# Expert 0's second-layer weights of the last MoE sent last, with two early weight pieces and four operations reordered

## The chip, the cores and the metric

The kernel runs on one core of a Trainium2 chip. The metric is the device time of one execution in microseconds (us); lower is better. The time before is the median of three runs. One further execution was profiled; all rows shown here come from it.

## What is computed

Three layers follow one another. An mLSTM attention runs over 4 batches x 8 heads x 768 tokens with head size 40, and its output is seen as x with 3072 rows and 320 columns. A first mixture of experts works on 32 slots, four for each of 8 experts. A second mixture of experts sends all 3072 rows through all 8 experts and adds them with Sinkhorn weights P.

```python
# first MoE (slots)
d = softmax_over_rows(x @ phi);  slot_input = d.T @ x          # 32 x 320
for e in range(E):
    slot_out[e] = np.maximum(slot_input[e] @ w1[e], 0) @ w2[e]  # 320 -> 1024 -> 320
x = softmax_over_cols(x @ phi) @ slot_out
# second MoE (all rows)
for e in range(E):
    out += P[:, e:e+1] * (np.maximum(x @ m2_w1[e], 0) @ m2_w2[e])
```

Each w1 or w2 of one expert is 320 x 1024 floats, 1.31 MB.

## The kernel before

The kernel has four stages. The attention loop `step` works through 24 tiles of 128 tokens, in an order written out by hand (`ORDER0`, `ORDER`); its last tiles follow `END`, and the way from the last tile to `siT`, the input of the first MoE's slots, follows `TAIL`. Then the first MoE's eight experts run one after another (`up`, `up_t`, `down`). What they give, `soT`, is multiplied with the second MoE's first-layer weights of expert 0 (`s1_p`, the product S); S is scaled by a power of two that comes from its largest magnitude (`pow2_s`) and split into two 16-bit halves (`s1_h`, `s1_l`), and from there on the second MoE runs as matmuls in 16 bits: `g1` gives a first-layer block z and its relu as two halves (hh by ScalarE, hl by VectorE), and `g2` multiplies them with the two 16-bit halves `wh` and `wl` of the second layer's weights. VectorE, ScalarE, GpSimd and TensorE keep the program's order wherever a `manual_schedule` is open. Here `man` holds TensorE throughout, and `man4` holds ScalarE, VectorE and GpSimd from expert 3 of the first MoE on.

The weights all come over SyncE's queue, in program order, into a ring of 15 places (`slot`): two buffers `wa`, three in `big`, two `bigx`, four `bigy`, four `wb`. A DMA is issued once its place is free and an earlier one, eight issues back, has landed. The attention loop sends the first pieces one at a time (`load_w(islice(ahead_parts, 1))`, by the list `WN`), `END` sends the rest of the first eleven matrices (entry `sl20`), and `load_n` sends the others in this order: `w20`, which is expert 0's w2 of the second MoE (n = 11), then the first MoE's matrices 11 to 15 with numbers shifted by one, then `m2w[0]`, the second MoE's w1 of expert 0. Behind them stand the second MoE's weights for experts 1 and 2.

`w20` goes through four steps, each in four quarters of 128 x 640: `amax` (VectorE, line 1091) finds the largest magnitude; `pow2_w` takes it over the partitions on GpSimd (line 1116) and makes a scale by four small VectorE operations (`pow2_b`, lines 1124 to 1132); `prep_a` (ScalarE, line 1149) writes the high half `wh`; and `prep_d` (VectorE, line 1153) the low half `wl`. All of that is woven into the first MoE's loop: `amax` beside experts 1 and 2, the scale at expert 3, and the halves beside experts 3 to 6.

In the code's names, `kk` is a quarter of w2, `kc` one of eight blocks of 128 hidden units, and a quarter of w2 serves two kc. S comes in four column blocks j, each of which serves two kc.

Of the kernel before, what the change touches and what calls it, by code (L numbers as in the profile page):

```python
# [20 lines left out]
def mlstm_moe_kernel(  # L21
# [46 lines left out]
    ORDER0 = "O KT KTa QT E0 E0a QTa E0g ST STd PC PK V E1 E1a E1g G0 DK CB DP US S W0 W1 YB"  # L68
    END = (
        "st sl20 s23 d20 w0 w1 x20 a20 lt4 tv4 n21 y21 g21 i22 v22 u22 i23 r22 v23 n22 y22 g22 x21 a21 q4 u23 x22 a22 r23 n23"  # L70
        " y23 e4 g23"
    )
    PB = [1, 2, 3]
    PD = 3
# [83 lines left out]
    def load_o(i0, i1):  # L158
        for i in range(i0, i1):
            b, c = divmod(i, NCH)  # L160
            nc.sync.dma_start(
                out=xs_(i).rearrange("p (h d) -> p h d", h=H),
                in_=o_gate[b, :, c * L:(c + 1) * L, :].rearrange("h p d -> p h d"),
            )
# [171 lines left out]
    def load_R(p):  # L336
        b, c = divmod(p * CPS, NCH)
        r0 = c // CPS * BH + b * H
        nc.sync.dma_start(out=Rt[p % 2][96:99, :, :], in_=gpd[r0:r0 + H, :, :].rearrange("r a s -> a r s"))
# [292 lines left out]
    def lt_a(gq):  # L632
        nc.scalar.activation(out=ct_all[:, gq], in_=ct_all[:, gq], func=AF.Exp)

    def lt_f(gq):
        ct = ct_all[:, gq]
        sm = late.tile([P, 4, 1], F32, tag="sm", name="sm")
        nc.vector.reduce_sum(out=sm, in_=ct, axis=AX.X)
        nc.vector.tensor_scalar_add(sm, sm, 1e-9)
        nc.vector.reciprocal(sm, sm)  # L640
        nc.vector.tensor_tensor(out=ct, in0=ct, in1=sm.to_broadcast([P, 4, NS]), op=ALU.mult)
# [33 lines left out]
    def load_w(parts):  # L675
        for d, s_ in parts:
            nc.sync.dma_start(out=d, in_=s_)
# [92 lines left out]
    k_a(1, 0, nc.vector)  # L770
    k_a(1, 1, nc.vector)
    load_o(0, 1)
    load_R(1)
    load_v(2)
    load_o(1, 2)
    load_w(islice(ahead_parts, 1))
    load_csa()
    e_g(0, 0)
    pr_k(0)
# [27 lines left out]
    SIG = {s: (s + 2, s + 3) for s in range(4, 22)} | {1: (1, 2), 2: (2, 4), 3: (4, 6)}  # L807
    OL = [4, 5, 6, 7] + list(range(8, NT)) + [NT] * NT
    LO = {i: (OL[i], OL[i + 1]) for i in range(NT + 1)}
    WN = [0, 1] * 8 + [1, 1, 1, 1, 0, 0]  # L810
    for i in range(NT - 2):
        step(i)
    def end():
# [45 lines left out]

    def load_n(n):  # L860

        if n < NRA:
            load_w(m1_parts(n))
        elif n == NRA:
            w20[0] = slot(n)
            load_w(w2_parts(w20[0], m2_w2, 0))
        elif n < 2 * E + 1:
            load_w(m1_parts(n - 1, n))
        elif n == 2 * E + 1:
            m2w[0] = slot(n)  # L870
            load_w(w1_parts(m2w[0], m2_w1, 0))

    for n in range(NRA, NR):
        load_n(n)
# [104 lines left out]
    def wk():  # L979
# [2 lines left out]
            nc.tensor.matmul(wm, ident16, ident16.unsqueeze(1).to_broadcast([P, 4, L]), start=True, stop=True)  # L982

    TAIL = (
        "x23p 0p x23a 0a lp 0d wk ld la mxp ls tp mxd wk tv mbp 1p mbd mba sp lc fwd sd 1a ftp tq ftd 1d te 2p 2a 2d 3p 3a 3d"
        " ltd4 ltf4 ltd lta ltf"
    )
    ops = dict(
        wk=wk, ltd4=lambda: (lt_d(gl - 1), lt_a(gl - 1)), ltf4=lambda: lt_f(gl - 1),
        x23p=lambda: x_p(NT - 1), x23a=lambda: x_a(NT - 1), lp=lambda: lg_p(gl), ld=lambda: lg_d(gl),  # L990
        la=lambda: lg_a(gl, 1), lc=lambda: lg_a(gl, 0), ls=lambda: lg_s(gl),
        tp=lambda: lt_p(gl, (1,)), tq=lambda: lt_p(gl, (0,)), tv=lambda: lt_v(gl, 1), te=lambda: lt_v(gl, 0), mxp=mx_p, mxd=mx_d,
        mbp=mb_p, mbd=mb_d, mba=mb_a, fwd=fw_d, sp=lambda: sl_p(gl), sd=lambda: sl_d(gl), ftp=ft_p, ftd=ft_d,
        ltd=lambda: lt_d(gl), lta=lambda: lt_a(gl), ltf=lambda: lt_f(gl),
    )
    for gq in range(len(cbk)):
        ops[f"{gq}p"] = lambda gq=gq: c_p(gq, *cbk[gq])
# [95 lines left out]
            axis=AX.X, op=ALU.max, apply_absolute_value=True,  # L1093
        )

    SPLIT = ((1, 0), (1, 1), (2, 1))

    def pow2(e, a, mx, later=None):

# [70 lines left out]
    mxg = sm_p.tile([P, 1], F32, name="mxg")  # L1170
    nc.vector.memset(mxg, 0.0)
    sg = sgs[:, 3 * NS:3 * NS + E]
    src2[0] = w20[0].rearrange("p (k d) -> p k d", d=DM)
    up(0)
    for e in range(E - 1):
        if e == 3:

            man4 = tc.manual_schedule(engines={mybir.EngineType.Activation, mybir.EngineType.DVE, mybir.EngineType.Pool})
            man4.__enter__()
        up_t(e)  # L1180
        up(e + 1)
        down(e)
        load_n(NR + 2 * e)
        load_n(NR + 2 * e + 1)
        if e < 3:
            if e < 2:
                c_p(4 + e, psp, "p")
                c_a(4 + e)
                c_d(4 + e)
            if e:  # L1190
                for kk in range(2 * e - 2, 2 * e):
                    amax(0, kk)
        else:
            if e == 3:
                pow2_w(0)
                c_m()
            prep_a(0, e - 3)
            prep_d(0, e - 3)

    def warm2(n):  # L1200
        pw2 = psz.tile([P, TB], F32, tag="z", name="pw2").rearrange("p (a l) -> p a l", a=4)
# [12 lines left out]
        nc.vector.tensor_copy(o, pt[64 * a:64 * a + 64, 2 * NS:3 * NS])  # L1214
    warm2(2)

    Sst = {}

    def s1_p(e):
# [19 lines left out]
    def s1_c(e, j):  # L1239
        s1_h(e, j)  # L1240
        s1_l(e, j)
# [10 lines left out]
    for kt, (o, n) in enumerate(KS):  # L1252
# [2 lines left out]
            start=(kt == 0), stop=(kt == 2), tile_position=(0, 0),  # L1255
        )
    warm2(10)
    pow2_s(0)

    def sg_s():  # L1260
        nc.vector.tensor_reduce(
# [144 lines left out]
    G1K = 3  # L1406

    s1_c(0, 0)
    g1(0, 0)
    s1_h(0, 1)  # L1410
    g1(0, 1)
    s1_l(0, 1)
    warm2(2)
    for kc in range(KF):
        for tt in range(TPB - 1):
            g2(0, tt, kc, kc + 1)
            if tt == 0 and 0 < kc < KF - 2:
                g1(0, kc + 2)
        if kc == 0:
            s1_h(0, 2)  # L1420
            g1(0, 2)
            s1_l(0, 2)
        elif kc == 1:
            s1_c(0, 3)
        if kc == 2:
            sg_s()
        elif kc == 3:
            sg_c()
        elif kc in (4, 5):
            gate_p(kc - 4)  # L1430
            gate_a(kc - 4)
        elif kc in (6, 7):
            gate_t(kc - 6)
            gate_d(kc - 6)
        if kc >= G1K:
            g1(1, kc - G1K)
# [442 lines left out]
```

## Time and profile before

| what | value |
|---|---|
| median of 3 runs | 875.19 us (874.96 to 876.23) |
| profiled execution | 873.51 us |
| its span, first to last instruction | 871.8 us |
| TensorE matmuls busy | 855.0 us, 98% of the span |
| VectorE, ScalarE, GpSimd busy | 694.4, 598.2, 635.8 us |
| data moved | 67.10 MB, mean 77 GB/s |

The shares are averages over stages with different limits: the DMA engines are full in the first 190 us and nearly idle after, and the time of one stage is read from the wait that ends last in that stage. Times in the rows count from the span's first instruction.

### The profile page before, as it was taken

The numbers are of one execution on the slowest core, as the hardware profiler recorded it, in microseconds if no ns is written. First come the engines' busy times: TensorE is split into PE (matmuls) and PEld (weight loads), VectorE is DVE, ScalarE is ACT, GpSimd is POOL, SyncE is SP. The second block draws the span as 40 slices with busy tenths as digits, with TensorE's granted clock in tenths as the row PEclk, the third lists the DMA queues.
The fourth block names the chain that finished last, engine by engine and source line by source line (L and its number), as shares of the span: only waits on it lengthen the run. The fifth ranks groups of instructions, "written<-read, shape, count | busy, mean of one in ns | idle before, by whom it ended". The sixth has DMA issues, their size and how long they took to land.

```text
span 871.8 us, 27361 instructions
## 1 busy us (share of the span) xinstructions
PE 855.0 (98%) x11320; PEld 739.5 (85%) x11320; DVE 694.4 (80%) x1558; ACT 598.2 (69%) x1233; POOL 635.8 (73%) x641
## 2 busy tenths in 40 slices
PE   7999997999999999999999999999999999999998
PEld 5888884446667998999999899999989998999997
DVE  7777876545887788888988888889887978787986
ACT  7565653444376988787778677867777777777773
POOL 4766661000055898988899888988899888899994
PEclk9999999999999999999999999999999999999999
DMA  8999999970101010302030202021201000000112
GB/s 175 194 188 187 193 241 313 329 233 1 61 1 62 2 62 20 66 2 62 20 65 2 64 24 60 2 65 45 37 9 58 17 5 2 5 17 17 54 48 70
DMA packets 136118, 67.10 MB, mean 77 GB/s; under 512 B 105049, under 2 KB 129753, under 8 KB 135993
## 3 DMA queue, kind: packets, MB, share of 16 engines
q1 hardware_dynamic: 135721, 64.86, 29.8%
q8 instruction: 89, 1.46, 0.7%
q14 instruction: 36, 0.29, 0.2%
q0 software_dynamic: 48, 0.20, 0.1%
q10 hardware_dynamic: 224, 0.30, 0.1%
HBM read 60.10 MB, written 5.02 MB: 75 GB/s over the span
## 4 chain that ended last, share of the span: by engine, by line
PE 87%; DMA 6%; DVE 3%; ACT 2%; SPq 1%; issue 0%; POOL 0%; ACTq 0%; POOLq 0%; DVEq 0%
PE y L1570 15%; PE z L1536 9%; DMA bigy<-in_moe_w_dram 3%; PE pss L432 3%; PE oa L477 2%; PE ptk L383 2%; PE y L1321 2%; PE y L1322 2%; PE y L1323 2%; DMA wa<-in_moe_w_dram 1%; PE pe L402 1%; PE ob L488 1%; PE z L1300 1%; DMA big<-in_moe_w_dram 1%; DMA wb<-in_moe_w_dram 1%; PE pu L1017 1%
## 5 line engine op out<-in xcount | busy, mean ns | idle before, releaser
L1548 POOL TENSOR_TENSOR op<-tm,op 128x512 f16<-128x512 f32 x325 | 370.1, 1161 | 55.3 <-ACT op L1617 49.5
L1667 PEld LDWEIGHTS <-op 128*128 128x128 f16 x5460 | 382.9, 98 | 1.5
L1617 ACT CAST op<-tm 128x512 f16<-128x512 f32 x325 | 197.1, 616 | 23.3 <-POOL tm L1626 21.3
L1545 DVE SCALAR_TENSOR_TENSOR tm<-z,tm 128x512 f32<-128x512 f32 x213 | 145.5, 683 | 68.4 <-ACT op L1542 63.4
L1570 PE MATMUL y<-wx,ch 128*128 128x320 f16 x912 | 139.6, 299 | 0.0
L1536 PE MATMUL z<-cst,sst 96*128 96x128 f16 x1344 | 130.8, 219 | 0.2 <-DVE tm L1545 0.2
L1542 ACT ACTIVATE tm<-z 128x512 f32<-128x512 f32 x130 | 76.6, 599 | 50.1 <-PE z L1536 41.7
L1570 PEld LDWEIGHTS <-ch 128*128 128x128 f16 x912 | 84.9, 97 | 27.9
L1536 PEld LDWEIGHTS <-sst 96*128 96x128 f16 x1344 | 96.3, 98 | 9.6 <-issue 2.5
L1542 ACT ACTIVATE op<-z 128x512 f16<-128x512 f32 x130 | 77.7, 598 | 26.0 <-PE z L1536 26.0
L1545 DVE SCALAR_TENSOR_TENSOR op<-z,op 128x512 f16<-128x512 f32 x130 | 88.3, 679 | 3.0 <-ACT op L1542 3.0
L1626 POOL TENSOR_TENSOR tm<-tm 128x512 f32<-128x512 f32 x47 | 59.7, 1271 | 5.4 <-ACT tm L1542 5.4
L1545 DVE SCALAR_TENSOR_TENSOR ch<-z,ch 128x512 f16<-128x512 f32 x76 | 51.9, 683 | 14.1 <-ACT ch L1542 14.1
L1542 ACT ACTIVATE ch<-z 128x512 f16<-128x512 f32 x76 | 45.2, 595 | 14.1 <-PE z L1536 14.0
L411 ACT ACTIVATE dd<-pe 128x512 f32<-128x512 f32 x48 | 29.3, 609 | 29.0 <-PE pe L402 28.6
L1323 PE MATMUL y<-wh,hl 128*128 128x320 f16 x160 | 47.8, 299 | 0.3 <-DVE hl L1304 0.3
L1321 PE MATMUL y<-wh,hh 128*128 128x320 f16 x160 | 47.8, 299 | 0.0
L1322 PE MATMUL y<-wl,hh 128*128 128x320 f16 x160 | 47.8, 299 | 0.0
L1116 POOL PARTITION_ALL_REDUCE mr<-mx x3 | 1.1, 383 | 63.7 <-DVE mx L1091 36.8
L1304 DVE SCALAR_TENSOR_TENSOR hl<-z,hh 128x512 f16<-128x512 f32 x48 | 31.2, 684 | 18.6 <-ACT hh L1303 18.5
L1451 POOL TENSOR_TENSOR wx<-raw,wx 128x640 f16<-128x640 f32 x28 | 39.2, 1403 | 8.0 <-ACT sst L1229 6.8
L1472 POOL TENSOR_TENSOR raw<-raw 128x640 f32<-128x640 f32 x28 | 43.3, 1548 | 0.2
(1201 smaller groups left out, 1750.5 us busy)
## 6 DMA issues: line engine op xcount, KB each, us to landing
wa<-in_moe_w_dram SPq DMA_DIRECT2D x18, 512.0 KB, 10.9
raw<-in_moe_w_dram SPq DMA_DIRECT2D x28, 320.0 KB, 4.7
kq<-in_k_dram SPq DMA_DIRECT2D x24, 160.0 KB, 3.9
kq<-in_q_dram SPq DMA_DIRECT2D x24, 160.0 KB, 4.5
vz<-in_v_dram SPq DMA_DIRECT2D x24, 160.0 KB, 3.4
xr<-in_o_gate_dram SPq DMA_DIRECT2D x24, 160.0 KB, 3.6
wb<-in_moe_w_dram SPq DMA_DIRECT2D x6, 640.0 KB
out_dram<-acc SPq DMA_DIRECT2D x24, 160.0 KB, 1.8
```

Source lines behind the costliest of these rows:

```text
L1321: nc.tensor.matmul(y, hh[:, kc, ts], wh[e][:, kc, :], start=(kc == 0), stop=False)
L1322: nc.tensor.matmul(y, hh[:, kc, ts], wl[e][:, kc, :], start=False, stop=False)
L1323: nc.tensor.matmul(y, hl[:, kc, ts], wh[e][:, kc, :], start=False, stop=(kc == KF - 1))
L1472: nc.gpsimd.tensor_tensor(out=quarter(e, *o), in0=quarter(e, *a), in1=quarter(e, *b), op=op)
L1536: nc.tensor.matmul(z[:, k, :], Sst[e][:, kc * P:(kc + 1) * P], cst[:, i * P:(i + 1) * P], start=True, stop=True,)
L1542: nc.scalar.activation(out=o, in_=z, func=AF.Relu)
L1545: nc.vector.scalar_tensor_tensor(out=o, in0=z, scalar=0.0, in1=x, op0=ALU.max, op1=op)
L1548: nc.gpsimd.tensor_tensor(out=o, in0=x, in1=h, op=ALU.subtract)
L1570: nc.tensor.matmul(self.y, self.at(a, kc), b[self.e][:, kc, :], start=(kc == a == 0 and b is wh), stop=(kc == KF - 1 and a == 1),)
L1617: cast = lambda m, x: nc.scalar.copy(out=hi(m), in_=x)
L1626: at(0, lambda: nc.gpsimd.tensor_tensor(out=s1_, in0=r21, in1=r22, op=ALU.add), 1)
L1667: nc.tensor.matmul(t[:, c * DH:(c + 1) * DH], o[:, m, a, kp, :], b[kp], start=(kp == a == 0 and b is bh), stop=(kp == KH - 1 and a == 1),)
```

## The change

Expert 0's w2 of the second MoE, `w20`, goes to the end of the row: `load_n` now sends the first MoE's matrices 11 to 15 in their own places, then `m2w[0]`, then `w20`. Its four steps leave the first MoE's loop. The first two `amax` stand behind the copies of `soT`, the third between the product S and `pow2_s`, the fourth and `pow2_w` behind `pow2_s`, and the closing operations of both scales behind them (`SPLIT` puts them off until they are called). `prep_a` and `prep_d` stand beside the blocks of S and the first z. `man4` is open from the first expert on.

One weight piece of the start is sent ahead of `load_R(1)`, `load_v(2)` and `load_o(1, 2)` rather than behind them, and the loop sends one more piece at step 2 (`WN`). In `END` the last tile's scaling `g23` goes ahead of the accumulation `e4`. In `TAIL` the copy `0d` goes behind `mxd`, and `sp` goes ahead of `1p`; the softmax of the last two logit groups (`lt_a`, `lt_f`) leaves `TAIL` and goes behind `up_t(0)`.

```diff
-        " y23 e4 g23"
+        " y23 g23 e4"
...
+    load_w(islice(ahead_parts, 1))
     load_R(1)
     load_v(2)
     load_o(1, 2)
-    load_w(islice(ahead_parts, 1))
     load_csa()
...
-    WN = [0, 1] * 8 + [1, 1, 1, 1, 0, 0]
+    WN = [0, 1, 1, 1] + [0, 1] * 6 + [1, 1, 1, 1, 0, 0]
...
-        if n < NRA:
+        if n < 2 * E:
             load_w(m1_parts(n))
-        elif n == NRA:
+        elif n == 2 * E:
+            m2w[0] = slot(n)
+            load_w(w1_parts(m2w[0], m2_w1, 0))
+        elif n == 2 * E + 1:
             w20[0] = slot(n)
             load_w(w2_parts(w20[0], m2_w2, 0))
-        elif n < 2 * E + 1:
-            load_w(m1_parts(n - 1, n))
-        elif n == 2 * E + 1:
-            m2w[0] = slot(n)
-            load_w(w1_parts(m2w[0], m2_w1, 0))
...
     TAIL = (
-        "x23p 0p x23a 0a lp 0d wk ld la mxp ls tp mxd wk tv mbp 1p mbd mba sp lc fwd sd 1a ftp tq ftd 1d te 2p 2a 2d 3p 3a 3d"
-        " ltd4 ltf4 ltd lta ltf"
+        "x23p 0p x23a 0a lp wk ld la mxp ls tp mxd 0d wk tv mbp sp 1p mbd mba lc fwd sd 1a ftp tq ftd 1d te 2p 2a 2d 3p 3a 3d"
+        " ltd4 ltd"
     )
...
-    SPLIT = ((1, 0), (1, 1), (2, 1))
+    SPLIT = ((0, 0), (0, 1), (1, 0), (1, 1), (2, 1))
...
-    src2[0] = w20[0].rearrange("p (k d) -> p k d", d=DM)
+    man4 = tc.manual_schedule(engines={mybir.EngineType.Activation, mybir.EngineType.DVE, mybir.EngineType.Pool})
+    man4.__enter__()
     up(0)
     for e in range(E - 1):
-        if e == 3:
-
-            man4 = tc.manual_schedule(engines={mybir.EngineType.Activation, mybir.EngineType.DVE, mybir.EngineType.Pool})
-            man4.__enter__()
         up_t(e)
+        if e == 0:
+            for gq in (gl - 1, gl):
+                lt_a(gq)
+                lt_f(gq, pb)
         up(e + 1)
         down(e)
         load_n(NR + 2 * e)
         load_n(NR + 2 * e + 1)
-        if e < 3:
-            if e < 2:
-                c_p(4 + e, psp, "p")
-                c_a(4 + e)
-                c_d(4 + e)
-            if e:
-                for kk in range(2 * e - 2, 2 * e):
-                    amax(0, kk)
-        else:
-            if e == 3:
-                pow2_w(0)
-                c_m()
-            prep_a(0, e - 3)
-            prep_d(0, e - 3)
+        if e == 1:
+            src2[0] = w20[0].rearrange("p (k d) -> p k d", d=DM)
+        if e < 2:
+            c_p(4 + e, psp, "p")
+            c_a(4 + e)
+            c_d(4 + e)
+        elif e == 3:
+            c_m()
...
     warm2(2)
 
+    amax(0, 0)
+    amax(0, 1)
     Sst = {}
...
     warm2(10)
+    amax(0, 2)
     pow2_s(0)
+    amax(0, 3)
+    pow2_w(0)
+    tmp.pop(("b", 0, 0))()
+    tmp.pop(("b", 0, 1))()
...
     s1_c(0, 0)
+    prep_a(0, 0)
     g1(0, 0)
+    prep_d(0, 0)
     s1_h(0, 1)
     g1(0, 1)
     s1_l(0, 1)
+    prep_a(0, 1)
+    prep_d(0, 1)
     warm2(2)
...
             s1_l(0, 2)
+            prep_a(0, 2)
+            prep_d(0, 2)
         elif kc == 1:
             s1_c(0, 3)
+            prep_a(0, 3)
+            prep_d(0, 3)
```

## Rows read from the trace of the kernel before

**Rows 1.** The span in stretches: busy us (instructions) by engine, clock, DMA share, GB/s.

```profile
core 0: us, PE busy (x) PEld busy (x) DVE busy (x) ACT busy (x) POOL busy (x), PEclk, DMA share, GB/s
165.00:175.00 10.00, 9.09 (x120) 3.71 (x112) 4.74 (x7) 5.41 (x11) 0.00 (x0) 1.00 1.06 316
175.00:180.00 5.00, 4.89 (x46) 1.90 (x42) 1.24 (x5) 0.00 (x0) 0.00 (x0) 1.00 1.05 305
190.00:195.00 5.00, 5.00 (x33) 2.98 (x32) 3.72 (x12) 3.32 (x8) 0.35 (x1) 1.00 0.06 20
400.00:860.00 460.00, 459.99 (x6192) 429.97 (x6189) 388.77 (x834) 343.78 (x697) 416.61 (x353) 1.00 0.12 34
```

**Rows 2.** Chain that ended last, 150 to 182 us: start, us, what.

```profile
150.86 7.40 DMA wb<-in_moe_w_dram
158.28 12.95 DMA wa<-in_moe_w_dram
171.25 8.93 DMA big<-in_moe_w_dram
180.42 0.77 PE pu L1023 x8
181.21 0.43 DVE mxs L1141
```

**Rows 3.** Timeline 182 to 194 us: start, us, engine, line, operation [idle before <-releaser].

```profile
182.14 0.15 DVE L1126 TENSOR_SCALAR iv<-mr 128x1 int32<-128x1 int32 x1 [0.51 <-POOL mr L1116]
182.76 0.47 ACT L1229 ACTIVATE sst<-pu,sc 32x256 f16<-32x256 f32 x1 [8.16 <-DVE sc L1132]
183.26 0.40 ACT L1237 COPY sst<-sst 32x256 f16<-32x256 f16 x1
184.30 0.60 ACT L1303 ACTIVATE hh<-z 128x512 f16<-128x512 f32 x1 [0.63 <-PE z L1300]
184.93 0.69 DVE L1304 SCALAR_TENSOR_TENSOR hl<-z,hh 128x512 f16<-128x512 f32 x1 [1.19 <-ACT hh L1303]
...
186.75 0.48 DVE L1233 SCALAR_TENSOR_TENSOR sst<-pu,sc,sst 32x256 f16<-32x256 f32 x1
191.21 0.69 DVE L1304 SCALAR_TENSOR_TENSOR hl<-z,hh 128x512 f16<-128x512 f32 x1 [0.35 <-ACT hh L1303]
193.66 0.21 DVE L1271 SCALAR_TENSOR_TENSOR sgs<-pg,sc,sgs 32x8 f16<-32x8 f32 x1
193.93 1.04 PE L1344 MATMUL pgl<-cst,sgs 96*128 96x512 f16 x4
```

**Rows 4.** What reads w20's place: count, ns min/median/max, first and last start.

```profile
L1091 DVE TENSOR_REDUCE mx<-wb x4: 809/809/819, 159.5 to 162.1; 128x1 f32<-128x640 f32 x4
L1149 ACT ACTIVATE wh<-wb,sc x4: 819/824/827, 165.1 to 173.1; 128x640 f16<-128x640 f32 x4
L1153 DVE SCALAR_TENSOR_TENSOR wl<-wb,sc,wh x4: 876/876/884, 165.9 to 174.3; 128x640 f16<-128x640 f32 x4
```

**Rows 5.** Timeline of SyncE's queue where END sends the rest of the weights.

```profile
118.34 0.63 SPq L677 DMA_DIRECT2D big<-in_moe_w_dram  x1
...
121.85 0.86 SPq L677 DMA_DIRECT2D big<-in_moe_w_dram  x1
```

**Rows 6.** Timeline from the attention's last tile to the first expert.

```profile
136.72 0.55 DVE L658 SCALAR_TENSOR_TENSOR sacc<-sacc,sc,pq 128x321 f32<-128x321 f32 x1
137.81 0.51 PE L552 MATMUL ptx<-ident,xr 128*112 128x128 f32 x3 [1.61 <-DVE mxg L1171]
139.46 0.68 DVE L889 SCALAR_TENSOR_TENSOR cst<-ptc,cst 32x512 f16<-32x512 f32 x1 [1.67 <-ACT cst L883]
142.23 0.61 PE L879 MATMUL ptc<-ident,ct_all 128*32 128x128 f32 x4
149.68 0.44 PE L1042 MATMUL pth<-ident,h 128*128 128x128 f32 x2 [1.83 <-DVE sm L638]
```

**Rows 7.** Stretches of 4 us around the first expert, for the clock.

```profile
148.00:152.00 4.00, 2.32 (x22) 1.23 (x26) 3.00 (x12) 1.26 (x4) 0.00 (x0) 0.77 1.00 265
152.00:156.00 4.00, 4.00 (x50) 1.97 (x46) 1.35 (x4) 1.22 (x3) 0.00 (x0) 0.81 1.04 358
```

**Rows 8.** TensorE's filling matmuls between S and the first z.

```profile
181.26 2.33 PE L1203 MATMUL pw<-ident 128*128 128x512 f16 x10
```

More of the change, by code (lines that the diff above doesn't have):

```diff
@@ L633, in lt_a, with lt_f @@
         nc.scalar.activation(out=ct_all[:, gq], in_=ct_all[:, gq], func=AF.Exp)
-    def lt_f(gq):
+    def lt_f(gq, pool=None):
         ct = ct_all[:, gq]
-        sm = late.tile([P, 4, 1], F32, tag="sm", name="sm")
+        sm = (pool or late).tile([P, 4, 1], F32, tag="sm", name="sm")
         nc.vector.reduce_sum(out=sm, in_=ct, axis=AX.X)
@@ L984, in mlstm_moe_kernel @@
     TAIL = (
-        "x23p 0p x23a 0a lp 0d wk ld la mxp ls tp mxd wk tv mbp 1p mbd mba sp lc fwd sd 1a ftp tq ftd 1d te 2p 2a 2d 3p 3a 3d"
-        " ltd4 ltf4 ltd lta ltf"
+        "x23p 0p x23a 0a lp wk ld la mxp ls tp mxd 0d wk tv mbp sp 1p mbd mba lc fwd sd 1a ftp tq ftd 1d te 2p 2a 2d 3p 3a 3d"
+        " ltd4 ltd"
     )
     ops = dict(
-        wk=wk, ltd4=lambda: (lt_d(gl - 1), lt_a(gl - 1)), ltf4=lambda: lt_f(gl - 1),
+        wk=wk, ltd4=lambda: lt_d(gl - 1),
         x23p=lambda: x_p(NT - 1), x23a=lambda: x_a(NT - 1), lp=lambda: lg_p(gl), ld=lambda: lg_d(gl),
@@ L993, in mlstm_moe_kernel @@
         mbp=mb_p, mbd=mb_d, mba=mb_a, fwd=fw_d, sp=lambda: sl_p(gl), sd=lambda: sl_d(gl), ftp=ft_p, ftd=ft_d,
-        ltd=lambda: lt_d(gl), lta=lambda: lt_a(gl), ltf=lambda: lt_f(gl),
+        ltd=lambda: lt_d(gl),
     )
```

## Prediction

> **What bounds the kernel now.** I read the stretches first, then the chain of waits, then the timeline of the place where the change works. From 190 us on TensorE has no idle time worth naming: 5.00 of 5 us between 190 and 195, 459.99 of 460 between 400 and 860 [rows 1]. Whatever delays or advances that run of matmuls moves the end by the same amount. Before it, up to 180 us, the DMA engines are the limit: their share stands at 1.05 and 1.06 (the measure of a full set here) and they move 305 to 316 GB/s [rows 1]. The chain says the same: it goes from weight to weight, `wb`, `wa`, `big`, the last of which is `m2w[0]`, landed at 171.25 + 8.93 = 180.2 us; only then do the last eight matmuls of S run (180.42) and the search for its largest magnitude (181.21) [rows 2]. So the second MoE begins when the last byte of a row of weights has come, and the compute of the first MoE is hidden behind that row.
>
> From S on there is a third limit. VectorE and ScalarE pass S through its halves, z, hh and hl; the first hl starts at 184.93 and the fifth ends at 191.21 + 0.69 = 191.90. The chain goes on to the gate's operand `sgs`, which ends at 193.87, and the gate product, which stands in TensorE's order behind the fifth block, starts at 193.93 [rows 3]. So a delay of VectorE's order here is carried to the end whole.
>
> **The row of weights.** `w20` was the first of the last seven matrices and becomes the last. Nothing is taken out of the row: 1.31 MB at 305 to 316 GB/s [rows 1] is 4.1 to 4.3 us, call it 4.2. The first MoE's matrices and `m2w[0]` land 4.2 us sooner, and `w20` lands where `m2w[0]` landed, at 180.2. What shortens the row is the extra piece at step 2. The loop then ends one piece further on, and the piece that `END` no longer sends is the last 128 KB of matrix 4, the row at 121.85 [rows 5]. Its data are 0.13 MB, 0.4 us; its issue took 0.86 us ahead of the rest, so the row can also begin up to 0.9 us sooner. I take 0.6, between the two, and `w20` lands at 179.6. The piece moved ahead of `load_R(1)` only changes places within the first 13 us; `load_R(1)`, `load_v(2)`, `load_o(1, 2)` and `load_csa` stand behind it on SyncE for one issue of 0.6 us (the row at 118.34 [rows 5]), and all of them are read several us later. I price it at nothing, from -0.3 to +0.3.
>
> **The tail's four moves.** `g23` ahead of `e4` takes the 0.55 us of the accumulation off TensorE's wait of 1.61 us. `0d` put off takes up to 0.68 from the path to `ld`, of which I count 0.4, since the logits' product ends inside it. `sp` ahead of `1p` saves about 0.55 of the 0.61 us of the transposes. `lt_a` and `lt_f` moved out take away most of the 1.83 us that `up_t(0)` waited [rows 6]. That is 0.55 + 0.4 + 0.55 = 1.5 us to `siT` and some 1.3 more to `up_t(0)`. I price all of it at nothing: the cover is the row of weights, which lands at its own pace, and the first MoE ends on it before and after. If that cover went, these moves would be worth up to 2.8 us. The earlier start of `man4` leaves the same short operations in the same loop and is hidden by the same cover.
>
> **The halves of w2, now behind the landing.** Before, the four `amax`, `prep_a` and `prep_d` ran between 159.5 and 175 us [rows 4], while the weights were awaited, and cost nothing. Now VectorE's order decides: the third `amax` stands ahead of S's own search, and it reads the second half of `w20`. So S, whose product could be ready by about 176.5, is held on VectorE until `w20` has landed. Behind that `amax` are queued S's search, its scale, every sst and every hl. From the landing at 179.6, with 0.1 for the semaphore:
>
> `amax` 0.81, to 180.5 [rows 4]; S's search 0.43, to 180.9 [rows 2]; the fourth `amax` 0.81, to 181.7, while GpSimd takes S's largest over the partitions; three small operations, of which the row at 182.14 is the first, 0.2 each, to 182.3; sst on ScalarE 0.47 and its copy 0.40, to 183.3 [rows 3]; `prep_a` 0.82, to 184.1 [rows 4] (the w2 scale's four small operations have ended by 183.1); hh 0.60, to 184.7; so the first hl starts at 184.8 against 184.93 [rows 3]. S's own matmuls (0.77) no longer lie behind the last landing, but two `amax` and a `prep_a` do, and they eat what the landing and the matmuls give.
>
> From there to the end of the fifth hl VectorE did 5 hl of 0.69 and 3 sst of 0.48, 4.89 us, in 191.90 - 184.93 = 6.97 us, so it waited 2.08 us [rows 3]. The change puts four `prep_d` of 0.88, 3.52 us, between them [rows 4]. If they all fit into the waits first, it takes 4.89 + 3.52 = 8.41; if none does, 6.97 + 3.52 = 10.49. I laid the two orders side by side, ScalarE's with four `prep_a` of 0.82 and VectorE's, each operation starting when its engine is free and its operand is there. The waits that stay are 0.65 us (before the second, third and fourth `prep_d` or hl, each of which waits for a `prep_a` or an hh). That gives 9.05 us, and the fifth hl ends at 184.8 + 9.05 = 193.85 against 191.90: 1.95 us later, by the bounds from 1.3 to 3.4. TensorE and the gate product follow.
>
> **The clock.** TensorE's product S now ends near 177 and the ten filling matmuls, 2.33 us [rows 8], near 179.5; the first z comes at 183.9. That leaves 4.4 us idle, where it was 0.3. After the idle 1.83 us ahead of 149.68 [rows 6] the granted clock read 0.77 and 0.81 in two stretches of 4 us [rows 7]: (0.46 + 0.38) x 4 = 3.4 us at 1.2 in place of 2.4 GHz. The Trainium skill, in "TensorE: Matmul & The Clock Gate", Part 1 on the HAM clock gate, says that half rate is the resting state and that activity releases it; by that rule the longer pause is paid for with a slower start of the second MoE, a charge against this change. By the rows, such a fall beside VectorE's chain costs 0.2 us, since TensorE waits there anyway, and up to 1.7 (half of 3.4) if it reaches into the full stretch. I take 0.25.
>
> **The sum.** 1.95 + 0.25 = 2.2 us. On the profiled execution the span goes from 871.8 to 874.0, and 873.51 to 875.7. The median of the runs lies 1.7 above the profiled time; on it the forecast is 875.19 + 2.2 = 877.4 us.
>
> **The rivals.** *The halves are absorbed.* If `w20` lands 1 to 2 us sooner than the order of the row says (a faster stretch of the DMA, a row that starts sooner), or VectorE's waits swallow nearly all of `prep_d`, the shift falls by the same amount: it is zero at a landing of 177.4. For it speak the 0.86 us of the issue and the 2.08 us of waits; against it, that the DMA share shows no gap. From +0.0 to +1.6: 875.2 to 876.8, with 876 in the middle.
>
> *Faster: S is not held by w20.* If `w20`'s second half were there when S is, S's search would start 4.2 + 0.6 us sooner, at 176.4; through the fourth `amax`, the scale, sst, copy, `prep_a` and hh (4.3 us by the rows above) the first hl would start at 180.7, and the fifth end at 189.75, 2.15 before 191.90: 873.0. It decides from a landing before about 175.5. For it: the tail is shorter, and fewer bytes wait behind. Against it: 1.31 MB cannot pass in no time on full engines.
>
> *The clock falls longer*, or VectorE's waits do not shrink (10.49): +3.2 to +3.9, 878.4 to 879.1.
>
> **How the numbers follow.** Forecast 877.4, with its own range 876.9 to 878.2: 0.47. Absorbed: 0.29. Longer fall or no overlap: 0.14. S not held: 0.10. For 8 in 10 the range goes from 874.2, in the gap between the faster case and the absorbed one, to 879.0. A measurement of this kernel tells about 0.2% from no change, 1.75 us: below 873.44 is faster, above 876.94 slower. Faster takes the case S not held, 0.10. Within 0.2% takes the absorbed case, 0.29, and a little of the forecast's lower edge, 0.02. Slower has the rest, 0.59.
>
> **What would show it.** In the profile after, the third `amax` should start at a DMA's landing near 179.7 and S's search right behind it, with S's matmuls done by 177; were the search started by TensorE instead, the forecast's first step is wrong. The fifth hl should end near 193.9 and `sgs` near 195.8. DMA share should stay above 1.0 up to the landing; a gap there would mean that the row was not the limit. `siT` should be 1.5 us sooner with no effect on the end, and matmuls from 195 on should be as many and as long as before.

## The result and the profile after

The changed kernel takes 880.35 us in the median (879.21 to 881.68), the kernel before, run beside it, 875.51 (874.96 to 876.23): slower by 4.8 us, where 2.2 were forecast, and above the top of the range, 879.0. The ratio on record is 1.0065 [1.0045, 1.0085]; it is not the quotient of these two medians, 1.0055, and taken by itself it would be 5.7 us. The profiled execution of after took 880.01 us with a span of 878.2; the one of before had 873.51 and 871.8.

In the two profiled executions all of the difference lies in the first 200 us. From the start of the gate product to the end of the span both traces need the same: 871.81 - 193.93 = 677.88 us before [rows 3], and 878.21 - 200.32 = 677.89 after. Stretches of after, with the columns of [rows 1]:

```profile
core 0: us, PE busy (x) PEld busy (x) DVE busy (x) ACT busy (x) POOL busy (x), PEclk, DMA share, GB/s
16.00:20.00 4.00, 3.75 (x56) 2.48 (x54) 3.30 (x11) 3.12 (x6) 2.94 (x7) 1.00 0.33 73
44.00:48.00 4.00, 2.75 (x74) 2.27 (x72) 1.61 (x5) 1.71 (x4) 1.31 (x2) 1.00 0.94 209
48.00:52.00 4.00, 2.64 (x36) 2.31 (x29) 2.54 (x8) 1.45 (x4) 0.98 (x2) 1.00 1.10 215
184.00:188.00 4.00, 0.83 (x4) 0.32 (x4) 2.74 (x11) 2.11 (x4) 0.76 (x2) 0.96 1.09 253
188.00:192.00 4.00, 3.09 (x12) 1.57 (x11) 3.45 (x5) 2.94 (x6) 0.00 (x0) 0.50 1.07 362
320.00:860.00 540.00, 539.80 (x7239) 502.27 (x7237) 456.71 (x978) 409.76 (x833) 488.15 (x413) 1.00 0.12 34
```

The last row is the second MoE: TensorE is full, as before. Two places are not. At 184 to 192 us, where the second MoE starts, TensorE is nearly empty for one stretch and then runs at a granted clock of 0.50, which is 1.2 GHz. And in the attention loop the DMA engines stand at a share of 0.33 at 16 to 20 us, and TensorE has holes at 44 to 52 us. The first two of these stretches before:

```profile
16.00:20.00 4.00, 3.75 (x56) 2.51 (x56) 3.33 (x11) 3.13 (x6) 2.95 (x7) 1.00 0.96 214
44.00:48.00 4.00, 4.00 (x94) 3.56 (x89) 2.59 (x7) 2.07 (x6) 2.00 (x3) 1.00 1.02 179
```

The chain of waits of after, where [rows 2] has the chain of before:

```profile
171.86 11.39 DMA big<-in_moe_w_dram
183.27 0.82 DVE mx L1089
184.12 0.42 DVE mxs L1139
```

The chain goes from the landing of `w20`'s second half (183.25) to the third `amax`, and S's search stands right behind it, as the forecast said. It said 179.6 for the landing. The timeline of after from S to the gate product, to be held against [rows 3]:

```profile
180.04 0.75 PE L1021 MATMUL pu<-wa,soT 128*32 128x256 f32 x8 [0.51 <-DMA wa<-in_moe_w_dram]
181.58 2.51 DVE L1089 TENSOR_REDUCE mx<-big 128x1 f32<-128x640 f32 x3 [3.09 <-DMA big<-in_moe_w_dram]
184.12 0.42 DVE L1139 TENSOR_REDUCE mxs<-pu 128x1 f32<-128x256 f32 x1
187.17 0.59 PE L1300 MATMUL z<-cst,sst 96*128 96x512 f16 x2 [3.96 <-DVE sst L1228]
188.21 0.69 DVE L1304 SCALAR_TENSOR_TENSOR hl<-z,hh 128x512 f16<-128x512 f32 x1 [1.19 <-ACT hh L1303]
191.84 0.63 PE L1300 MATMUL z<-cst,sst 96*128 96x512 f16 x1
193.13 0.69 DVE L1304 SCALAR_TENSOR_TENSOR hl<-z,hh 128x512 f16<-128x512 f32 x1 [1.43 <-ACT hh L1303]
197.58 0.69 DVE L1304 SCALAR_TENSOR_TENSOR hl<-z,hh 128x512 f16<-128x512 f32 x1
200.32 1.04 PE L1344 MATMUL pgl<-cst,sgs 96*128 96x512 f16 x4 [0.64 <-DVE sgs L1271]
```

S's matmuls end at 180.8, its search starts at 184.12. TensorE waits 3.96 us for the first z. The z at 191.84 takes 0.63 us, where one takes 0.38 at full clock (195.22 in the same trace). From the first hl to the gate product it is 12.11 us, against 193.93 - 184.93 = 9.00 before [rows 3].

Two distances split the 6.39 us between the two gate products. From S's search to the gate product: 200.32 - 184.12 = 16.20 us, against 193.93 - 181.21 = 12.72 before, so **3.48 us behind S's search**. And S's search itself comes 2.91 us later. The loop and SyncE's queue show what could make it late. SyncE of after, and the matmuls of TensorE that waited for a DMA:

```profile
10.97 0.57 SPq L677 DMA_DIRECT2D wa<-in_moe_w_dram  x1
16.95 1.28 SPq L297 DMA_DIRECT2D csa<-cpd  x3
35.91 1.41 SPq L677 DMA_DIRECT2D wa<-in_moe_w_dram  x1
38.59 3.46 SPq L363 DMA_DIRECT2D phi_sb<-in_moe_phi_dram  x2
43.35 0.38 SPq L156 DMA_DIRECT2D vz<-in_v_dram  x1
...
46.27 1.13 PE L477 MATMUL oa<-vz,dd 128*64 128x41 f32 x32 [1.25 <-DMA vz<-in_v_dram]
50.65 0.39 PE L402 MATMUL pe<-R,csl 99*128 99x512 bf16 x1 [1.36 <-DMA R<-gpd]
```

`csa` is read back from `cpd`, so its issue waits on SyncE until the write of `cpd` has landed, and SyncE's queue stands still with it. The same places in the kernel before:

```profile
12.84 1.05 SPq L677 DMA_DIRECT2D wa<-in_moe_w_dram  x1
14.77 1.28 SPq L297 DMA_DIRECT2D csa<-cpd  x3
36.58 0.39 SPq L156 DMA_DIRECT2D vz<-in_v_dram  x1
```

With the piece of `wa` ahead, `csa` goes out 2.2 us later, and SyncE issues nothing from 12.96 to 16.95; the share of 0.33 stands right behind that. The second piece, 640 KB at 35.91, goes ahead of `phi_sb` and of this `vz`, which is 6.8 us later than before, and TensorE waits for it and for R. Not all of that belongs to the pieces: the trace of before is the quickest of all in this part. In the kernels below that have neither piece early, `phi_sb` goes out at 36.5 to 38.3 us too and this `vz` at 38.1 to 40.4, and TensorE waits for R in all of them (0.2 to 1.7 us). Only its wait of 1.0 to 1.5 us for `vz`, at 46 us in after, stands in the three traces with both pieces alone. In the loop, the attention products `pss` (line 432) of the first and the eighth tile lie 54.04 - 14.79 = 39.25 us apart after, and 50.35 - 14.76 = 35.59 before.

### The profile page after: what moved, and what is told of

The parts are those of the page before. It is cut to its first block, busy times and chain, and to the rows that moved or that the text cites. A ratio compares the mean times of both kernels' runs of the same rounds, so it can differ in the third digit from the quotient of the medians.

```text
span 878.2 us, 27365 instructions
## 1 busy us (share of the span) xinstructions
PE 856.8 (98%) x11320; PEld 740.1 (84%) x11320; DVE 694.7 (79%) x1558; ACT 598.5 (68%) x1233; POOL 635.6 (72%) x641
## 4 chain that ended last, share of the span: by engine, by line
PE 87%; DMA 6%; DVE 3%; ACT 2%; issue 1%; SPq 1%; POOL 0%; ACTq 0%; DVEq 0%
PE y L1578 15%; PE z L1544 9%; PE pss L432 2%; PE y L1322 2%; PE y L1323 2%; PE y L1321 2%; PE oa L477 2%; PE ptk L383 2%; DMA wb<-in_moe_w_dram 2%; DMA big<-in_moe_w_dram 1%; PE pe L402 1%; PE ob L488 1%; PE z L1300 1%; DMA bigy<-in_moe_w_dram 1%; DMA bigx<-in_moe_w_dram 1%; PE pu L1015 1%
## 5 line engine op out<-in xcount | busy, mean ns | idle before, releaser
L439 DVE TENSOR_TENSOR dd<-pss,dd 128x512 f32<-128x512 f32 x48 | 30.9, 685 | 15.2 <-PE pss L432 12.4
```

## The experiments

Each kernel was timed beside the kernel before on the same chip. Single runs of the kernel before lie between 872.3 and 880.1 us over all chips, so the ratios on record are compared, and inside a trace only distances between two events of it. The column in us is the ratio times the median of the kernel before on that chip.

| kernel | ratio to before [95%] | us | first z to gate product |
|---|---|---|---|
| changed, first timing | 1.0065 [1.0045, 1.0085] | +5.7 (medians: +4.8) | 13.15 |
| e8, changed, once more | 1.0056 [1.0035, 1.0077] | +4.9 | 13.37 |
| e2, changed without pieces | 1.0042 [1.0026, 1.0057] | +3.7 | 13.38 |
| e5, e2 and more filling | 1.0039 [1.0024, 1.0054] | +3.4 | 12.01 |
| e13, w20 third last | 1.0041 [1.0026, 1.0056] | +3.6 | 12.82 |
| e6, S ahead of amax | 1.0042 [1.0028, 1.0056] | +3.7 | 16.78 |
| e9, e6 and filling | 1.0034 [1.0017, 1.0052] | +3.0 | 15.71 |
| e1, before and both pieces | 1.0013 [0.9996, 1.0030] | +1.1 | 10.04 |
| e3, before and start piece | 1.0022 [1.0005, 1.0039] | +1.9 | 10.04 |
| e11, before and step 2's piece | 1.0014 [0.9997, 1.0030] | +1.2 | 10.03 |
| e10, before, csa first | 1.0018 [1.0000, 1.0037] | +1.6 | 10.04 |
| e4, before and tail's moves | 0.9995 [0.9978, 1.0012] | -0.4 | 10.04 |
| e7, before and late pieces | 0.9996 [0.9986, 1.0006] | -0.4 | 10.04 |
| e12, tail, csa first, late pieces | 1.0015 [0.9998, 1.0033] | +1.3 | 10.04 |
| e14, w20 not loaded | 0.9962 [0.9947, 0.9978] | -3.3 | 10.05 |

The last column, from one trace each, splits the kernels into two kinds: wherever the halves of `w20` are made ahead of S, it is 10.03 to 10.05 us, and 12 us or more where they are made behind it. In e6 and e9 the first z itself comes sooner, so their distance does not compare with the others. e8 is the changed kernel once more, beside e5, e6 and e7; 4 to 5.5 us and a slip of 2 to 5 us in the loop were expected, and it shows 4.9 and 40.30 - 35.59 = 4.7.

**The three parts alone.** e1 is the kernel before with both early pieces, e2 the changed kernel without them, e4 the kernel before with the tail's moves.

```
e1:  +    load_w(islice(ahead_parts, 1))   # ahead of load_R(1), not behind load_o(1, 2)
     +    WN = [0, 1, 1, 1] + [0, 1] * 6 + [1, 1, 1, 1, 0, 0]
e2:  the changed kernel with these two lines as before
e4:  the kernel before with END, TAIL, lt_a and lt_f as in the changed kernel
```

> The kernel before with the two early weight pieces alone (one ahead of load_R(1), one more at step 2). Theory: the pieces go in front of the attention's own loads and make TensorE wait for them; the sixth and seventh product S of the attention loop slip by 3.7 us, as in the changed kernel, the row of weights starts 3 us later and ends 2.5 to 3.3 us later, and the time is 2.5 to 3.7 us above before. Rival (the slip of the loop is not the pieces' doing): 0 within 0.5 us, or 0.5 us faster by the shorter row.

> The changed kernel with both early pieces put back. Theory: the attention loop runs as before (no slip at its seventh step), w20 lands near 180.2, and what is left is the chain behind the landing with a lower clock: 2 to 3.3 us above before. Rival (pieces harmless): 4 to 5 us above before, as the changed kernel. Second rival (w20's late halves harmless): within 0.5 us of before.

> The kernel before with the four reordered operations alone (g23 before e4, 0d behind mxd, sp before 1p, lt_a and lt_f behind up_t(0)). Theory: siT is ready about 1.5 us sooner, m2w[0] still lands at 180.2, and the time is that of before within 0.4 us. Rival: the first MoE's start counts and the time falls by 1 to 2.5 us.

e2 keeps +3.7 us [2.3, 5.0], between the 2 to 3.3 expected and the rival's 4 to 5, with an interval that reaches into both: the late `w20` with its halves is the larger part. e2 also has the earlier `man4`, which no run takes alone; but its trace has 16.43 us from S's search to the gate product, 3.7 more than before, and `man4` is open there in both. e1 gives +1.1 [-0.4, +2.6], less than the 2.5 to 3.7 expected, and e8 against e2, on two chips, 4.9 - 3.7 = 1.2: the pieces are the smaller part, and neither number alone is clear of zero. e4 is not told from before: relative to the last `pss`, `siT` comes at 15.9 us where it was 17.2, 1.3 sooner, and the time does not follow. The parts add to 3.7 + 1.1 - 0.4 = 4.4, where the changed kernel has 4.9 (e8) and 5.7 (4.8 by the medians).

**Which piece.** e3 has the start's piece alone, e11 the piece of step 2 alone, and e7 sends three more pieces late instead.

```
e3:   the first line of e1          e11:  the second line of e1
e7:  -    WN = [0, 1] * 8 + [1, 1, 1, 1, 0, 0]
     +    WN = [0, 1] * 8 + [1, 1, 1, 1, 3, 0]
```

> The kernel before with only the piece at the start sent ahead of load_R(1), load_v(2) and load_o(1, 2). Theory, if the stall of SyncE's queue ahead of load_csa is half of the loss: 1 to 2 us slower, with load_csa issued at 17 in place of 14.8 us. If the piece at step 2 is all of it: 0 within 0.3 us. If the start piece is all of it: 3 to 3.7 us.

> The kernel before with the list WN of the changed one: one 640 KB piece more at step 2, and nothing else. If this piece delays the loop's own loads on SyncE's queue, as the trace of the changed kernel shows (phi issued 4.8 us later, TensorE waiting for vz and R), the eighth product S comes 2 to 3 us later behind the first than the 35.6 of the kernel before, and csa stays near 15 us; the time rises by 0 to 1 us, since the row of weights behind the loop gets 0.1 MB back. If the start's piece alone made the loop late, the distance stays within 0.5 us of 35.6 and the time within 0.5 us of the kernel before.

> The kernel before with three more pieces sent in step 20, while SyncE's queue waits for TensorE to free v's buffer. Theory (the row of weights is the limit, and its gaps cost): the row ends up to 1 us sooner and the time falls by 0.3 to 1 us. Rival (the gaps there are covered by loads already in flight): same within 0.3 us.

In e3 `csa` goes out at 16.76, as in after; in e11 at 14.74, as before. From the first to the eighth `pss` it is 37.41 us in e3 and 37.61 in e11, 39.25 to 40.35 in the three traces with both pieces, 35.59 in before and 36.2 to 38.2 in the kernels with neither in its early place (e2, e4 to e7, e9, e10, e12 to e14). So both pieces together stand out of the scatter in the loop, one alone does not. The 2.0 us by which e11's loop is later than that of before is what was expected of it, but e10, without a piece in an early place, has 37.59 too. TensorE's wait for R, 1.24 us in e11, is no mark of the piece either: it is 1.68 in e10.

By the ratios e3 is slower (+1.9 [+0.4, +3.4]) and e11 not told from before (+1.2 [-0.3, +2.6]). e3 stands above e1, which contains its edit; were that real, the piece of step 2 would gain 0.8 us, and e11 shows no gain. So it is the size of what these timings leave open. Late pieces (e7) are not told from before either.

**Why csa was late.** e10 moves `load_csa` ahead of the start's piece.

```
e10:      load_o(1, 2)
     +    load_csa()
          load_w(islice(ahead_parts, 1))
     -    load_csa()
```

> The kernel before with load_csa ahead of the start's piece of wa. Theory A, that the 512 KB piece in flight delays cpd's small write, which csa waits for: csa is issued before 14.0 us (14.8 in the kernel before, 16.9 in the changed one), the piece behind it by 15.5, and the eighth product S of the loop 35.6 us or less behind the first. The time is that of the kernel before, or up to 1 us below. Theory B, that cpd's write takes this long by itself: csa stays at 14.5 to 15.0, the piece goes out at 16, and the row of weights starts 2 to 3 us later with the time up to 1 us above.

```profile
12.01 0.31 ACTq L286 DMA_DIRECT2D cpd<-gbuf  x1
14.84 1.28 SPq L297 DMA_DIRECT2D csa<-cpd  x3
```

`cpd` is written from ScalarE's queue at 12.01, and `csa` goes out at 14.84, as in the kernel before, although no piece was in flight. So theory B holds for the write: it needs 2.8 us here by itself, 2.7 in before, where a piece was issued 0.8 us behind it (12.84), and 4.9 in after, where one was issued ahead of it (10.97, `cpd` at 12.07). The order of the kernel before used this wait for the piece; e10 leaves the queue empty in it and gains nothing (+1.6 [0.0, +3.2]).

**The clock.** e5 is e2 with 26 filling matmuls between S and the first z, not 10.

```
e5:  -    warm2(10)
     +    warm2(26)
```

> The changed kernel with both pieces put back, and 26 filling matmuls between S and the first z in place of 10, so that TensorE does not pause there. Theory (the lower clock lengthens VectorE's chain by 1 us, because each z waits behind slow matmuls): no fall of the clock between 183 and 195 us, first hl to start of the gate product 11.1 us in place of 12.1, and about 1 us faster than the kernel with the pieces put back (+3.4 us over before becomes +2.4). Rival (TensorE only waits there): the clock stays up and the stretch from first hl to gate product stays at 12.1 us.

```profile
187.85 0.59 PE L1300 MATMUL z<-cst,sst 96*128 96x512 f16 x2 [0.39 <-DVE sst L1228]
188.89 0.69 DVE L1304 SCALAR_TENSOR_TENSOR hl<-z,hh 128x512 f16<-128x512 f32 x1 [1.19 <-ACT hh L1303]
197.12 0.69 DVE L1304 SCALAR_TENSOR_TENSOR hl<-z,hh 128x512 f16<-128x512 f32 x1
199.86 1.04 PE L1344 MATMUL pgl<-cst,sgs 96*128 96x512 f16 x4 [0.65 <-DVE sgs L1271]
...
188.00:192.00 4.00, 2.76 (x16) 1.24 (x15) 3.06 (x5) 3.61 (x7) 0.00 (x0) 1.00 1.07 357
```

The pause ahead of the first z falls from 3.96 us in after to 0.39, the granted clock stays at 1.00, and from the first z to the gate product it is 12.01 us, not 13.15 as in after or 13.38 as in e2: the lower clock behind the pause costs 1.14 to 1.37 us there. The five hl take 197.12 + 0.69 - 188.89 = 8.92 us. The 11.1 us expected from the first hl to the gate product came (10.97); the gain of 1 us in the time did not. By the ratios e5 is 0.3 us below e2, with intervals of 1.3 us on either side. The granted clock on record, a mean over the whole run, is 0.990 to 0.992 in the eight runs of e2 and 0.996 to 0.998 in the six of e5, so the clock was up in all of them. But e5's profiled execution loses elsewhere more than it gains here: from the gate product to its end it needs 879.7 - 199.9 = 679.8 us, where before and after need 677.9, and the loss begins near 504 us, where ScalarE starts a `ch` 1.7 us later behind the gate product than in after though its z is done as soon, and ends in holes on TensorE:

```profile
504.76 0.60 ACT L1550 ACTIVATE ch<-z 128x512 f16<-128x512 f32 x1 [2.47 <-PE z L1544]
515.14 0.40 PE L1544 MATMUL z<-cst,sst 96*128 96x128 f16 x4 [0.86 <-DVE tm L1553]
```

Whether the other runs of e5 have this loss is not on record, so the timed runs neither confirm nor exclude what the lower clock costs in the trace.

**Is it the landing or the order?** e13 is e2 with `w20` sent three places from the end, ahead of matrix 15 and of `m2w[0]`, with the same order of its halves.

```
e13:  -        if n < 2 * E:
      +        if n < 2 * E - 1:
                   load_w(m1_parts(n))
      +        elif n == 2 * E - 1:
      +            w20[0] = slot(n + 2)
      +            load_w(w2_parts(w20[0], m2_w2, 0))
               elif n == 2 * E:
      -            m2w[0] = slot(n)
      +            load_w(m1_parts(n - 1))
      +        elif n == 2 * E + 1:
      +            m2w[0] = slot(n - 1)
      ...
```

> The changed kernel without its two early pieces, but with w20 sent three places from the end (ahead of the first MoE's matrix 15 and of m2w[0]), so that it lands some 2.62 MB or 8 us before the row ends; the order of its halves on VectorE, ScalarE and GpSimd is that of the changed kernel. Theory A, that the order of the halves costs about 2.4 us and S's wait for w20's landing adds about 1.1 by the pause of TensorE and its lower clock: S's search starts behind S's matmuls, TensorE's pause before the first z is below 2 us, the granted clock stays at 1.00 there, the gate product starts 12.0 us behind the first z as in e5, and the ratio to the kernel before is about 1.0027. Theory B, that the order alone makes all of it and the wait and the clock nothing: 13.2 us behind the first z and a ratio of 1.004. Theory C, that the landing of w20 is what costs and the order is hidden: 10 to 10.5 us and a ratio within 0.0005 of 1.

The timeline and one stretch of e13:

```profile
180.62 2.27 DVE L1091 TENSOR_REDUCE mx<-big 128x1 f32<-128x640 f32 x3
181.35 0.61 PE L1023 MATMUL pu<-wa,soT 128*32 128x256 f32 x8
182.92 0.42 DVE L1141 TENSOR_REDUCE mxs<-pu 128x1 f32<-128x256 f32 x1
185.97 0.59 PE L1302 MATMUL z<-cst,sst 96*128 96x512 f16 x2 [1.50 <-DVE sst L1230]
198.79 1.04 PE L1346 MATMUL pgl<-cst,sgs 96*128 96x512 f16 x4 [0.65 <-DVE sgs L1273]
...
184.00:188.00 4.00, 1.80 (x8) 0.43 (x6) 2.56 (x11) 3.27 (x6) 0.38 (x1) 1.00 1.06 358
188.00:192.00 4.00, 3.45 (x14) 1.81 (x14) 2.87 (x5) 2.79 (x6) 0.00 (x0) 0.62 0.72 244
```

No DMA holds the three `amax` any more (they start behind the copy of `soT`; `w20` had landed at 172.2, and the last piece of the row at 179.6), and the pause is 1.50 us. Still S's search waits, now for VectorE itself: S's matmuls end at 182.0, the three `amax` at 182.9. From 182.92 to 198.79, the gate product comes 15.87 us behind S's search, 0.33 less than in after and 0.56 less than in e2, and the time is e2's. This is theory B on the time and lies between A and B in the trace. So with `w20` landed 7 us ahead of the row's end, 15.87 - 12.72 = 3.15 us behind S's search are still lost: that is the order of the late halves, with the fall of the clock that comes with it, and not the landing. The equal time alone would not show it, as e13 is late ahead of S as well: matrix 15, now behind `w20`, holds the last product of the experts until 175.77, and that product takes 2.35 us where it takes 1.27 in after. And the clock fell all the same: TensorE was busy for 1.80 of 4 us at 184 to 188, while VectorE and ScalarE also made halves. Theory A had put the fall down to the pause ahead of the first z alone; that is wrong.

**S ahead of the amax.** e6 is e2 with S's search, its scale and the first block of S ahead of the four `amax`, two of which stand ahead of the second block's high half and two behind it, and with the halves of `w20` behind the second block; e9 adds filling matmuls in TensorE's pauses.

```
e6:  -    amax(0, 0)  amax(0, 1)      # behind the copies of soT
          warm2(10)
          pow2_s(0)
     ...
          s1_c(0, 0)
     +    amax(0, 0)
     +    amax(0, 1)
          g1(0, 0)
          s1_h(0, 1)
     +    amax(0, 2)
     +    amax(0, 3)
     +    pow2_w(0)
          g1(0, 1)
          s1_l(0, 1)
     ...                               # prep_a, prep_d, third block
e9:       g1(0, 1)
     +    warm2(17)
     ...
          g1(0, 2)
     +    warm2(4)
```

> The changed kernel with both pieces put back, and S's search, scale and first block ahead of the four amax on VectorE, so that S no longer waits for w20. Theory (S held by w20 plus the w2 operations on VectorE's order are the loss): S's search starts 4 us ahead of w20's landing, the gate product starts 13.5 to 14.5 us after the landing in place of 17.3, and the time is 2.5 to 3.5 us below that kernel, near before (within 0.8 us). Rival (the halves' place beside the blocks is the whole loss, S's wait none): at most 1 us better, 2.4 us above before.

> The kernel e6 (S not held by w20, no extra pieces) with 17 filling matmuls behind the second z and 4 behind the third, 21 x 0.22 = 4.6 us of TensorE's time in pauses of 4.1 and 0.9 us. Theory A, that e6 lost on its median what it gains in S because TensorE's pauses let the granted clock fall for one or more stretches in most runs: time at the lower clock falls by 3 us or more, and the ratio to the kernel before falls from e6's 1.0042 to between 1.000 and 1.002. Theory B, that the gate waits for w20's low halves, which end at the same distance behind the landing whether S is early or not: the ratio stays at 1.003 to 1.005, and the gate product starts 14 to 15 us behind the start of the last amax, as in e6. By both, the pauses of TensorE around 182 to 189 us are filled.

DVE and TensorE of e6:

```profile
179.14 0.42 DVE L1139 TENSOR_REDUCE mxs<-pu 128x1 f32<-128x256 f32 x1 [1.91 <-PE pu L1021]
183.90 1.53 DVE L1089 TENSOR_REDUCE mx<-big 128x1 f32<-128x640 f32 x2
186.67 0.59 PE L1294 MATMUL z<-cst,sst 96*128 96x512 f16 x1 [4.12 <-DVE sst L1226]
188.20 0.43 PE L1315 MATMUL y<-wh,hh 128*128 128x320 f16 x1 [0.94 <-ACT wh L1147]
198.74 0.61 PE L1338 MATMUL pgl<-cst,sgs 96*128 96x512 f16 x2 [0.53 <-DVE sgs L1265]
```

S's search is free of `w20` and comes right behind its matmuls. But `g2` needs `wh`, and `wh` needs the scale from all four `amax`: the first product with `wh` starts at 188.20, and the gate product 14.84 us behind the start of the last pair of `amax`. The wait has moved from S to `wh`. The theory of e6 fails with that: near before was expected, and the time is e2's, as the rival had it. With TensorE filled (e9) this distance is 198.91 - 185.15 = 13.76, and no clock fell in the stage. By the ratios neither is told from e2 (+3.7 and +3.0). The granted clock on record, again a mean over the run, is 0.990 to 0.996 in e6 and 0.994 to 1.000 in e9, so the filling raised it, as theory A of e9 wanted; but the ratio it expected, 1.000 to 1.002, lies at the edge of what was measured, 1.0034 [1.0017, 1.0052], where theory B's 1.003 to 1.005 lies inside; B's distance of 14 to 15 us became 13.76. So the clock is at most part of what keeps e6 slow. The profiled run of e6 was its fastest, 878.3 against a median of 881.5, so the trace does not show a typical run of it; what its typical run waits for stays open.

**Is the row the limit?** e14 is the kernel before without the load of `w20`; an older matrix stands in its place.

```
e14: -            w20[0] = slot(n)
     -            load_w(w2_parts(w20[0], m2_w2, 0))
     +            w20[0] = m1[n - 1]
```

> The kernel before without the load of w20: its halves are made from a first-MoE matrix that is there already, so 1.31 MB leave the row of weights, and the second MoE's output uses wrong weights for expert 0. Theory A, that the row is what ends last in every run: S's search comes 4.2 us sooner at 305 to 316 GB/s, and the time falls by 4 us (ratio 0.9952). Theory B, that the loop and the first MoE's own chain are close behind the row: the time falls by less than 2.5 us, and TensorE or VectorE, not a DMA, releases the last matmuls of S.

The end of its chain of waits (start, us, what):

```profile
175.35 1.28 PE pd L1052 x16
...
178.74 1.00 PE pu L1016 x16
179.77 0.77 PE pu L1022 x8
180.56 0.44 DVE mxs L1140
```

The time falls by 3.3 us [1.9, 4.6]; theory A's 4 lies inside the interval, theory B's "less than 2.5" too, so the time alone does not decide. The trace does: no DMA stands in the chain from 151 us on, and TensorE's own work for the experts ends last, as B said. So the row ends last in the kernel before, but the first MoE's compute lies only some 3 us ahead of its end.

**A better version?** e12 puts the tail's moves, `csa` first and the late pieces together.

```
e12: e4, e10 and e7 together
```

> The kernel before with the four moves of the tail, load_csa ahead of the start's piece, and three pieces more at step 20 in place of the row behind END; w20 stays first in the row. If the row of weights is all that counts, the moves of the tail give nothing, the late pieces up to 0.5 us, and csa first up to 0.5: from 0 to 1 us below the kernel before. If the order of the start is what it takes to start the row sooner, 1 us or more below.

It is not faster (+1.3 [-0.2, +2.9]), where 0 to 1 us below before, or more, were expected. No kernel here with the whole computation is faster than the kernel before beyond its interval.

## Why the prediction was wrong, point by point

The direction and the mechanism were right: `w20`'s landing released the third `amax`, S's search stood right behind it, and the order of VectorE behind that was the price. Without the early pieces (e2) the direction is the same, so it was no luck. The size was half of what came. Two terms of the sum were mis-sized: the early pieces, and the clock. Split at S's search, the forecast had 180.5 - 181.21 = -0.7 us ahead of it and, behind it, 0.58 to the first hl, 2.08 from there and 0.25 for the clock: 2.9. Measured in the traces are 3.48 behind it; what remains of the 4.84 us between the medians, 1.4, is put ahead of it (by the ratio on record it would be 2.2). The misses are 2.1 and 0.6 us; with 0.3 by which the second median of the kernel before is higher, they make the 3.0 us between 877.4 and 880.35.

**The row of weights and the early pieces (-0.7, was +1.4).** The start's piece was priced at nothing, because what stands behind it is read several us later. But `csa` is not a plain load: it waits for a small write, and a piece ahead of that write moves it from 14.77 to 16.95, with the engines at a share of 0.33 behind it; e3, which has this piece alone, is slower by 1.9 us [0.4, 3.4]. The step 2 piece was booked as a gain of 0.6 us; its 640 KB went ahead of `vz`, for which TensorE waited in the traces with both pieces, and no run shows the gain. Both pieces cost +1.1 [-0.4, +2.6] by e1 and 1.2 by e8 against e2, neither clear of zero alone; the 0.2 to 0.3 us that are left of the 1.4 are less than these runs can place. That the two pieces gain no 0.6 us is shown, as the interval of e1 lies above such a gain; what they cost is shown less well.

**The clock (0.25, was 1.14 in the trace).** The forecast reckoned that TensorE waits for VectorE there anyway. That does not hold where VectorE waits for a z in turn: at 191.84 a z took 0.63 us, and the hl behind it started at 193.13 after 1.43 us idle. Here the rule of the Trainium skill, "TensorE: Matmul & The Clock Gate", Part 1, that half rate is the resting state and activity releases it, agrees with the trace: the clock reads 0.50 at 188 to 192, after a stretch in which TensorE worked for 0.83 us of four. Nearest of the rivals came "the clock falls longer", with 878.4 to 879.1 us and a chance of 0.14: its mechanism is the one that the trace shows behind S, and it too left out what the pieces cost.

**What held.** S's matmuls were done 2.4 us ahead of the landing (180.8 against 183.25), where 2.6 were forecast. From the landing to the first hl 5.2 us were forecast and 4.96 measured (183.25 to 188.21); the 0.1 us booked in it for the semaphore was 0.02 in after (183.25 to 183.27). From the first hl to the end of the fifth 9.05 were forecast; it was 10.06 in after and 8.92 in e5, where the clock did not fall, so the layout of the two orders was right to 0.13 us. The tail's moves brought `siT` 1.3 us sooner in e4 (forecast 1.5) and nothing to the time, for the cover named. That the row ends last was right, but by e14 with a margin of some 3 us [1.9, 4.6] only. Of the rivals, "S is not held by `w20`" was built as e6: S's search did come with S's matmuls, but the rival overlooked that `wh` then holds `g2`, so its 873.0 us could not come about in that order.

**The landing itself.** It was forecast at 179.6 and was 183.25. About half of this is no cost of the change: 179.6 was counted from the landing in before's one profiled execution, and kernels with `w20` in its old place and no early pieces searched S at 187.74 (e4), 185.22 (e7), 186.19 (e10) and 184.51 (e12), where before has 181.21 [rows 2]. Before's profiled execution is 2.0 us below its median of 875.51, after's 0.3 below its own, which makes 1.7 of the 3.65 us. In the sum this did no harm, as it was carried to the median; as a mark to look for in the profile after it was too sharp.

**What stays open.** The share of the clock in the 3.7 us of the late halves rests on the traces (1.14 us); the timed runs of e5, with the clock up, do not show it. What the two pieces cost apart from each other is below what the timings resolve. And e6 and e9 are not told from e2 in the median, though their profiled runs reach the gate product at 198.74 and 198.91 against 200.99 in e2.

## What to carry to other kernels

A load that is moved up a queue must be priced at every dependent transfer that it now precedes, small DRAM round trips above all: look for an issue that waits on that queue, and for who waits behind it. Work that was hidden beside a wait for weights is not hidden because its own weights now land in that wait: it then stands on the engine that ends the stage, and its cost is there even if the weights come early (e13). A filling that removes a low clock is to be judged by the whole span and not by the stretch alone (e5). And the time at which a full DMA stage ends in one profiled execution is a draw; read the distance of that execution to the median as doubt on that stage before taking its landing as a term.

## What the runs showed of the hardware

The read of `cpd`, which waits for its write, was issued 2.7 to 3.3 us behind the issue of that write in the kernels with no weight piece ahead of it (2.7 in before, with one issued 0.8 us behind it, 2.8 in e10 with none), and 4.5 to 4.9 us behind it in the four where a 512 KB piece had been issued 0.8 to 1.1 us ahead. In the stretch from 16 to 20 us the DMA engines then moved 73 to 110 GB/s, where they moved 214 in before and 183 to 237 in the others.

The granted clock fell not only behind an unbroken pause (3.96 us in after, 4.12 in e6) but also in e13, where the longest pause from S to the fall was 1.50 us and TensorE was busy for 1.80 us in the stretch of 4 us before the fall; in e9, with the pauses filled, it stayed at 1.00 from 176 to 202.
